# A float32 decode attention block on one core: from a tile framework with five 4 MB buffers to hand-written engine programs with two 8 MB buffers and a TensorE loop

## The chip, the core and the metric

One NeuronCore of a Trainium2 chip runs the kernel: TensorE (PE, with its weight loads listed as PEld), VectorE (DVE), ScalarE (ACT), GpSimd (POOL), SyncE (SP, which here only issues DMAs) and 16 DMA engines. The metric is the device time in microseconds of one execution. Before the change it is 381.81 us (median of 3 runs, 381.46 to 384.05).

## The reference

One token per batch row (B = 2) is normalised, goes through grouped-query attention over a cache of 4096 keys, and its result is multiplied by a gate from a small feed-forward block:

```python
xn = _layernorm(x, axis=-1)
q = (xn @ wq).reshape(B, Sq, 16, 256).transpose(0, 2, 1, 3)
k = jnp.repeat(k_cache, 2, axis=1)      # 8 heads of K and V, 4096 x 256 each
v = jnp.repeat(v_cache, 2, axis=1)
scores = jnp.einsum("bhqd,bhkd->bhqk", q, k) * (256 ** -0.5)
o = jnp.einsum("bhqk,bhkd->bhqd", softmax(scores), v)
s = o.transpose(0, 2, 1, 3).reshape(B, Sq, 16 * 256) @ wo
g = silu(((xn @ w_gate) * (xn @ w_up)) @ w_down)
return x + s * g
```

Everything is float32. K and V are 16 pieces of 4 MB each (2 batch rows times 8 heads), 134 MB together; the weights are another 24 MB. Each byte is read once.

## The kernel before

The work is 16 steps, one for each head g and batch row b (`Step`, L156). A step has one K piece and one V piece, each a tile of 128 partitions by 8192 floats (32 KB rows), which `stream` (L38) loads into a ring of five such buffers through SP's queue. The weights `wq` (two halves), `wg`, `wu` and `wd` go through the same ring; `wo` has two small buffers of its own.

The stages of a step, with the names that the profile shows:

- `scores(h)` (L179 to L191): 8 matmuls of 512 columns for each half h of the keys into `s` (L187), in four groups of 32 output partitions; DVE takes the row maximum of each half (L190).
- `softmax` (L193): the maximum over partitions by a transpose (L197), a DVE reduce `mx` (L199) and a small matmul (L202); then ACT's two exponentials `p` (L207), and `sr`, the sums (L210).
- `turn` (L213): 8 transposes of `p` into `pt` (L218), copied to `pT` by DVE and ACT (L219), and the sums' matmul (L220).
- `values(h)` (L224): 16 matmuls of 256 columns for each half into `o` (L230), then ACT's copy `ob` (L234).
- `combine` (L236): two small matmuls (L239) and DVE's scaling into `oT` (L242).

A float32 matmul with 512 or 256 columns is two MATMUL and two LDWEIGHTS rows in the profile (1024 rows of L230 for 512 calls); a transpose is one of each.

The order of instructions on each engine is that of the code, since the pools run under a manual schedule. The main loop (L273 to L304) keeps two steps in flight: it issues the loads of V for step i and of K for step i + 2, then multiplies the first half of V of step i, puts the softmax of step i + 1 between the two halves, turns step i + 1's weights, and computes the scores of step i + 2 around `combine`. The gate's matmuls (`ffn_in`, `ffn_out`) lie in steps 1 and 2, the second half of q in step 4, and the projection `project` (L255) follows each finished head. The last V piece is loaded in smaller parts with the last parts of `wo` between and behind them (`load_v_last`, L166). A load waits on SP until its ring buffer has been read by TensorE.

## Time and profile before

| what | value |
|---|---|
| median of 3 runs | 381.81 us |
| the profiled execution: span from first to last instruction | 379.9 us |
| HBM bytes read | 158.54 MB, 417 GB/s over the span |
| TensorE busy, mean granted clock | 247.3 us (65%), 0.80 |
| DVE, ACT, POOL busy | 65.4, 44.2, 1.2 us |

The page gives no separate total for the profiled execution; its span is its own time, 1.9 us under the median of the runs, and that difference is taken as the part of a run that lies outside the first and last instruction. In rows of the profile, `x16` is a count of instructions, the first number of a timeline row is its start in us from the span's start and the second its length; what stands in square brackets is the idle time ahead of it and what ended that. "DMA share" is the mean busy share of the 16 DMA engines.

### The profile page before, as it was taken

What the parts mean: (1) busy time and instruction counts of PE and PEld (TensorE: products, weight loads), DVE (VectorE), ACT (ScalarE), POOL (GpSimd) and SP (SyncE); (2) the same over time, 40 slices, a digit from 0 to 9 for tenths busy, and PEclk for the clock granted to TensorE, in tenths of its full rate; (3) what the DMA queues carried; (4) which work ended last, traced back from release to release, by engine and by line L of the source; (5) the groups of instructions that cost most, each with busy time, mean ns of one, the idle gap of its engine ahead of it and who ended that gap; (6) DMA issues with size and microseconds to landing.
All of it is one profiled execution on the core that took longest, in us unless ns stands there. A gap on an engine that the chain in (4) does not pass through costs nothing.

```text
span 379.9 us, 5146 instructions
## 1 busy us (share of the span) xinstructions
PE 247.3 (65%) x2320; PEld 111.0 (29%) x2320; DVE 65.4 (17%) x173; ACT 44.2 (12%) x103; POOL 1.2 (0%) x7
## 2 busy tenths in 40 slices
PE   0648494939656684957676577767749474947585
PEld 0112241403341331423232233414314132413153
DVE  3032120101121020102101111111202111111120
ACT  1001020300130210201102020201002020202020
POOL 1000000000000000000000000000000000000000
PEclk9996686795898886758668886888867888698889
DMA  8999999999999999999999999999999999999992
GB/s 336 438 438 433 424 419 433 440 402 449 423 436 438 404 446 420 437 428 440 425 435 423 428 427 438 426 431 412 449 426 428 433 428 426 435 432 430 416 397 100
DMA packets 7690, 158.87 MB, mean 418 GB/s; under 512 B 882, under 2 KB 1396, under 8 KB 2932
## 3 DMA queue, kind: packets, MB, share of 16 engines
q1 hardware_dynamic: 7648, 158.54, 97.7%
q8 instruction: 18, 0.29, 0.3%
q14 instruction: 4, 0.03, 0.0%
q10 hardware_dynamic: 20, 0.01, 0.0%
HBM read 158.54 MB, written 0.00 MB: 417 GB/s over the span
## 4 chain that ended last, share of the span: by engine, by line
DMA 84%; PE 14%; DVE 1%; issue 0%; SPq 0%
DMA ring<-v 45%; DMA ring<-kt 34%; PE o L230 5%; PE s L187 5%; DMA ring<-wq 3%; PE s L90 2%; DMA wo<-wo 2%; PE o L239 1%; DVE mx L199 1%; PE s L93 1%; PE sm L202 0%; PE pt L218 0%; PE pt L108 0%; PE sm L197 0%; PE acc L259 0%
## 5 line engine op out<-in xcount | busy, mean ns | idle before, releaser
L230 PE MATMUL o<-ring,pT 128*32 128x256 f32 x1024 | 91.7, 519 | 62.4 <-DMA ring<-v 62.0
L187 PE MATMUL s<-ring,qT 128*32 128x512 f32 x512 | 86.6, 813 | 36.6 <-DMA ring<-kt 36.6
L230 PEld LDWEIGHTS o<-ring,pT 128*32 128x32 f32 x1024 | 42.1, 142 | 100.8 <-issue 90.3
L207 ACT ACTIVATE p<-s,m 128x512 f32<-128x512 f32 x32 | 21.7, 682 | 257.4 <-DVE m L203 257.4
L190 DVE TENSOR_REDUCE m<-s 128x1 f32<-128x512 f32 x32 | 22.1, 691 | 115.4 <-PE s L187 115.4
L187 PEld LDWEIGHTS s<-ring,qT 128*32 128x32 f32 x512 | 16.7, 132 | 71.4 <-issue 41.6
L199 DVE TENSOR_REDUCE mx<-sm 1x128 f32<-1x512 f32 x16 | 10.9, 679 | 108.6 <-PE sm L197 108.6
L218 PE MATMUL pt<-ident,p 128*128 128x128 f32 x128 | 18.3, 284 | 1.6 <-ACT p L207 1.6
L90 PE MATMUL s<-ring,xnT 128*32 128x512 f32 (+1 forms) x96 | 12.6, 664 | 7.5 <-DMA ring<-wq 6.2
L218 PEld LDWEIGHTS pt<-ident,p 128*128 128x128 f32 x128 | 14.0, 143 | 10.2 <-ACT p L207 6.4
L239 PEld LDWEIGHTS o<-sel,ob 128*128 128x128 f32 x64 | 10.7, 238 | 21.3 <-issue 20.3
L202 PE MATMUL sm<-one,mx 1*128 1x1 f32 x32 | 7.1, 287 | 12.3 <-DVE mx L199 12.3
L219 DVE COPY pT<-pt 128x512 f32<-128x512 f32 x16 | 11.0, 691 | 14.6 <-PE pt L218 14.6
L239 PE MATMUL o<-sel,ob 128*128 128x2 f32 x64 | 12.0, 292 | 0.5 <-ACT ob L234 0.5
L219 ACT COPY pT<-pt 128x512 f32<-128x512 f32 x16 | 9.4, 585 | 10.1 <-PE pt L218 10.1
L202 PEld LDWEIGHTS sm<-one,mx 1*128 1x128 f32 x32 | 5.7, 221 | 16.3 <-DVE mx L199 16.3
L259 PEld LDWEIGHTS acc<-wo,oT 128*32 128x32 f32 x256 | 7.8, 126 | 6.7 <-issue 5.8
L259 PE MATMUL acc<-wo,oT 128*32 128x112 f32 x256 | 9.3, 286 | 0.2 <-DMA wo<-wo 0.2
L210 DVE TENSOR_TENSOR sr<-su 128x128 f32<-128x128 f32 x16 | 4.7, 292 | 26.3 <-ACT p L207 26.3
L234 ACT COPY ob<-o 128x256 f32<-128x256 f32 x16 | 6.0, 372 | 16.8 <-PE o L230 16.8
L90 PEld LDWEIGHTS s<-ring,xnT 128*32 128x32 f32 x96 | 3.2, 123 | 14.1 <-issue 11.9
L207 ACT ACTIVATION_READ_ACCUMULATOR p<-s,m 128x1 f32 x32 | 6.3, 196 | 0.0
(52 smaller groups left out, 57.9 us busy)
## 6 DMA issues: line engine op xcount, KB each, us to landing
ring<-kt SPq DMA_DIRECT2D x16, 4096.0 KB, 44.5
ring<-v SPq DMA_DIRECT2D x15, 4096.0 KB, 44.7
ring<-wq SPq DMA_DIRECT2D x2, 3584.0 KB, 28.1
wo<-wo SPq DMA_DIRECT2D x6, 896.0 KB, 46.2
ring<-wg SPq DMA_DIRECT2D x1, 3136.0 KB
ring<-wu SPq DMA_DIRECT2D x1, 3136.0 KB, 38.7
ring<-wd SPq DMA_DIRECT2D x1, 3136.0 KB, 35.5
ring<-v SPq DMA_DIRECT2D x1, 2048.0 KB, 35.9
```

The source lines that it names most:

```text
L90: nc.tensor.matmul(ps[W * c:W * (c + 1), :n], xnT[:, k, :], block(NT * k + c), start=k == 0, stop=False)
L187: nc.tensor.matmul(s[W * c:W * (c + 1), :], qT[:, self.g, self.b, d].rearrange("p r j -> p (r j)"), k[:, d, c, :], start=d == 0, stop=d == 1)
L190: nc.vector.tensor_reduce(self.m[:, h:h + 1], s, axis=AX.X, op=OP.max)
L199: nc.vector.tensor_reduce(mx, sm[:1, None, :128].rearrange("p o (c j) -> p o j c", c=NT).to_broadcast([1, NT, W, NT]), axis=AX.X, op=OP.max)
L202: nc.tensor.matmul(sm[:, 128:129], mx.rearrange("p c j -> p (c j)"), one, start=True, stop=True)
L207: nc.scalar.activation(self.p[:, h], self.s[h], AF.Exp, bias=m[:, 3:4], scale=1.0 / 16, accum_out=su[:, h:h + 1])
L218: nc.tensor.transpose(pt[:, i, :], self.p[:, h, i * 128:(i + 1) * 128], ident)
L219: (nc.vector.tensor_copy, nc.scalar.copy)[h](self.pT[:, h], pt)
L230: nc.tensor.matmul(self.o[W * c:W * (c + 1), :DH], self.pT[:, h, i, W * c:W * (c + 1)], vt[:, i, c, :], start=h == 0 and i == 0, stop=h == ...
L234: nc.scalar.copy(self.ob, self.o[:, :DH])
L239: nc.tensor.matmul(oc[:, 2 * d:2 * d + 2], self.ob[:, d * 128:(d + 1) * 128], sel, start=True, stop=True)
L259: nc.tensor.matmul(acc[W * n:W * (n + 1), :], l, wo_t[g][:, i, n * SL:(n + 1) * SL], start=g == 0 and i == 0, stop=g == HKV - 1 and i == 3)
```

## The change

The kernel is written anew for each engine, with semaphores set by hand in place of the framework. What changes in the work:

- **Loads.** Two buffers `buf` of 128 x 16384 floats (64 KB rows) take the place of the ring of five. One load brings V of step i and K of step i + 2 as one 8 MB tile (`kv`); the first brings K of steps 0 and 1; V of steps 14 and 15 come as 4 MB tiles (`vv`). The load i into a buffer is issued when TensorE has done the scores of step i, the last work on that buffer.
- **Weights.** All of the feed-forward and q weights are loaded and used ahead of the first K, as three loads (50, 25 and 56 KB rows). All of `wo` is loaded at the end in six parts, behind the last V, and all of the projection follows the last step.
- **V's product.** Each matmul takes two neighbouring key blocks, 512 columns wide: 16 matmuls for a step in place of 32. Half of each product is not wanted; `join` picks the wanted half with four small matmuls in place of `combine`'s two.
- **Order.** TensorE's step is values, turn, join, scores, then the maximum's transpose and matmul, without the softmax in the middle of values. The maximum is one DVE reduce over 1024 columns. The query operand is spread out for each step by a POOL copy into `qs`.
- **Loop.** 14 of TensorE's 16 steps are a hardware loop of 7 turns with two steps in its body; the other engines' programs are written out.
- `take` is a wait followed by a decrement of the semaphore, an instruction of its own.

TensorE before, one step in the middle of the program (`o` is V's product, `sm` the small results, `s` the scores):

```order
L230 MATMUL o<-ring,pT 32x256 x16
L197 MATMUL sm<-ident,m 1x128
L202 MATMUL sm<-one,mx 128x1
L230 MATMUL o<-ring,pT 32x256 x16
L218 MATMUL pt<-ident,p 128x128 x8
L220 MATMUL sm<-sel,sr 128x2
L187 MATMUL s<-ring,qT 32x512 x8
L239 MATMUL o<-sel,ob 128x2 x2
L187 MATMUL s<-ring,qT 32x512 x8
```

TensorE after, one step of the loop's body:

```order
L366 MATMUL o<-buf,pT 32x512 x16
L300 MATMUL pt<-ident,p 128x128 x8
L356 MATMUL sm<-sel,sr 128x2
L374 MATMUL oc<-sel,ob 128x2 x4
L344 MATMUL s<-buf,qs 32x512 x16
L348 MATMUL sm<-ident,m 1x128
L350 MATMUL sm<-one,mx 128x1
```

V's product is one block, and the maximum's transpose and matmul have moved from its middle to the end of the step.

SP's queue before, the last part of the program (each K, V or `wo` load with what it waits for; the names are semaphores of the DMA queue and of TensorE):

```order
L40 DMA ring<-kt 128x8192 [waits DMAHW4_49,PE_49]
L40 DMA ring<-v 128x8192 [waits DMAHW5_49,PE_49]
L169 DMA ring<-v 128x4096 [waits DMAHW7_49,PE_49]
L174 DMA ring<-v 128x1024
L174 DMA ring<-v 128x1024 [waits DMAHW6_49]
L174 DMA ring<-v 128x1024
L253 DMA wo<-wo 128x896 [waits DMAHW0_49]
```

SP's queue after, from the first K to the last part of `wo`:

```order
L124 DMA buf<-kv 128x16384 [waits pe]
L127 DMA buf<-kv 128x16384 [waits pe] x14
L130 DMA buf<-vv 128x8192 [waits pe] x2
L133 DMA low<-wo 128x6272
L133 DMA low<-wo 128x4032
L133 DMA low<-wo 128x1792
```

Each load of the stream now waits for one event of TensorE, and all of `wo` stands behind the last of them, which waits for the scores of step 15.

The core of the diff:

```diff
-    ring = ctx.enter_context(tc.tile_pool(name="ring", bufs=5))
-    def stream(src, size=ROW):
-        t = ring.tile([128, ROW], F32, name="ring")
-        nc.sync.dma_start(t[:, :size], src)
-        return t[:, :size]
...
+LOOPS = 7
+WO = 4 * HKV
+ABREAST = (14, 9, 4)
+DIRECT = (3, 1, 1)
+    def take(self, sem, n=1):
+        self.e.wait_ge(sem, n).then_inc(sem, -n)
...
+    buf = [sb(f"buf{i}", [128, 2 * ROW]) for i in range(2)]
+    low = sb("low", [128, 28 * FC])
...
+    def dma_side():
+        e = nc.sync
+        e.dma_start(low, wgu).then_inc(sems["gu"], 16)
+        e.dma_start(buf[1][:, :14 * D], wd).then_inc(sems["wd"], 16)
+        e.dma_start(buf[0][:, :28 * 512], wq).then_inc(sems["wq"], 16)
+        sp.after(pe, "y4")
+        e.dma_start(buf[1], kv[0]).then_inc(turns[1], 16)
+        for i in range(N - 2):
+            sp.after(pe, *(("q", 1) if i == 0 else ("s", i)))
+            e.dma_start(buf[i % 2], kv[1 + i]).then_inc(turns[i % 2], 16)
+        for i in range(N - 2, N):
+            sp.after(pe, "s", i)
+            e.dma_start(buf[i % 2][:, :ROW], vv[i % 2]).then_inc(turns[i % 2], 16)
+        for n, lo, hi in zip(won, bounds, bounds[1:]):
+            t = low[:, lo * D:hi * D] if hi <= early else late[:, (lo - early) * D:(hi - early) * D]
+            e.dma_start(t, wo[:, lo * D:hi * D]).then_inc(n, 16)
+        sp.after(dv, "res")
+        e.dma_start(out, r1).then_inc(sems["res"], 16)
...
+        po.after(dv, "qT")
+        for i in range(N):
+            g, b = where(i)
+            if i >= 2:
+                po.after(pe, "s", i - 2)
+            e.tensor_copy(qs[i % 2], qT[:, g, b, :, None, :].to_broadcast([128, 2, DUP, REP])).then_inc(sems["q"], 1)
...
+        for i in range(N):
+            ac.after(pe, "v", i)
+            e.copy(ob, o).then_inc(sems["ob"], 1)
+            if i + 1 < N:
+                half(i + 1)
+            if i + 2 < N:
+                exps(i + 2)
...
+        def maximum(i):
+            dv.after(pe, "s", i)
+            e.tensor_reduce(m[:, 0:1], s.rearrange("p h n -> p (h n)"), axis=AX.X, op=OP.max).then_inc(sems["m"], 1)
+            dv.after(pe, "m", i)
+            e.tensor_reduce(
+                mx, sm[:1, None, :128].rearrange("p o (c j) -> p o j c", c=NT).to_broadcast([1, NT, W, NT]),
+                axis=AX.X, op=OP.max).then_inc(sems["mx"], 1)
+            dv.after(pe, "x", i)
+            dv.ev(e.tensor_scalar(m[:, 1:2], sm[:, 128:129], -1.0 / 16, None, op0=OP.mult), "neg", i)
...
+        for i in range(N):
+            if i + 1 < N:
+                half(i + 1)
+            heads(i)
+            if i + 2 < N:
+                maximum(i + 2)
...
+        def scores(i, k):
+            pe.take(sems["q"])
+            k = k.rearrange("p (h d c n) -> p h d c n", h=2, d=2, c=NT)
+            for h in range(2):
+                for d in range(2):
+                    for c in range(NT):
+                        ins = e.matmul(s[W * c:W * (c + 1), h], qs[i % 2][:, d].rearrange("p j q -> p (j q)"),
+                                       k[:, h, d, c, :], start=d == 0, stop=d == 1)
+            pe.ev(ins, "s", i)
+            pe.take(sems["m"])
+            pe.ev(e.transpose(sm[:1, :128], m[:, 0:1], ident), "m", i)
+            pe.take(sems["mx"])
+            pe.ev(e.matmul(sm[:, 128:129], mx.rearrange("p c j -> p (c j)"), one, start=True, stop=True), "x", i)
+
+        def turn(i):
+            pe.take(sems["sr"])
+            for h in range(2):
+                pe.ev(turned(pt[h], p[:, h]), "t", i, h)
+            pe.ev(e.matmul(sm[:, 130:132], sr, sel[:, 0], start=True, stop=True), "u", i)
+
+        def values(i, v):
+            pe.take(turns[i % 2], 16)
+            pe.take(sems["pt"], 2)
+            v = v.rearrange("p (h i c n) -> p h i c n", h=2, i=BLK, c=2)
+            for h in range(2):
+                for j in range(BLK):
+                    for c in range(2):
+                        at = 2 * (j % 2) + c
+                        ins = e.matmul(o[W * at:W * (at + 1), :], pT[:, h, j, 64 * c + 16:64 * c + 48],
+                                       v[:, h, j, c, :], start=h == 0 and j < 2, stop=h == 1 and j >= 2)
+            pe.ev(ins, "v", i)
+
+        def join(i):
+            pe.take(sems["ob"])
             for d in range(2):
+                for h in range(2):
+                    ins = e.matmul(oc[:, 2 * d:2 * d + 2], ob[:, h * 256 + d * 128:h * 256 + (d + 1) * 128], sel[:, h],
+                                   start=h == 0, stop=h == 1)
+            pe.ev(ins, "j", i)
+
+        pe.take(turns[1], 16)
+        scores(0, buf[1][:, :ROW])
+        turn(0)
+        scores(1, buf[1][:, ROW:])
+
+        at, count = dict(pe.at), pe.n
+        with nc.Fori(0, LOOPS, 1, engines=[PE], head_slot={PE: 0}):
+            for i in range(2):
+                values(i, buf[i][:, :ROW])
+                turn(i + 1)
+                join(i)
+                scores(i + 2, buf[i][:, ROW:])
...
+        i = N - 2
+        values(i, buf[0][:, :ROW])
+        turn(i + 1)
+        join(i)
+        values(i + 1, buf[1][:, :ROW])
+        pe.after(dv, "oT", i)
+        join(i + 1)
+        pe.after(dv, "gate")
...
+        for n, lo, hi in zip(won, bounds, bounds[1:]):
+            e.wait_ge(n, 16)
             for i in range(lo, hi):
+                if i >= 4 * (HKV - 1):
+                    pe.after(dv, "oT", N - 1)
+                if i < early:
+                    ins = abreast(o, left(i), wo_step(i), i, early)
+                else:
+                    for c in range(NT):
+                        ins = e.matmul(acc[W * c:W * (c + 1), :SL], left(i), wo_step(i)[:, c * SL:(c + 1) * SL],
+                                       start=False, stop=i == WO - 1)
+            if hi == early:
+                pe.ev(ins, "w4")
+                pe.after(ac, "accs")
+                spread(False)
+        pe.ev(ins, "fin")
...
-    kt = c(k.transpose(0, 1, 7, 3, 6, 5, 4, 2)).reshape(B, HKV, 128, ROW)
-    v = c(A_v_cache).reshape(B, HKV, 128, ROW)
+    k = k.transpose(1, 0, 7, 3, 6, 5, 4, 2).reshape(N, 128, ROW)
+    v = np.asarray(A_v_cache).transpose(1, 0, 2, 3).reshape(N, 128, ROW)
+    kv = np.concatenate([np.concatenate([k[:1], v[:N - 2]]), k[1:]], 2)
+    vv = c(v[N - 2:])
...
+    wq = np.concatenate([folded(wq[:, h * 2048:(h + 1) * 2048], 512) for h in range(2)], 1)
+    wo = c(np.asarray(A_wo).reshape(WO, 128, D).transpose(1, 0, 2)).reshape(128, WO * D)
+    wgu = np.concatenate([folded(np.asarray(w), FC) for w in (B_w_gate, B_w_up)], 1)
```

## The prediction

> **What bounds the kernel now.** I read the page first (span, DMA queues, chain of waits, DMA issues), then the busy time by stretches, then SP's waits.

> ```profile
> span 379.9 us, 5146 instructions
> ...
> PE 247.3 (65%) x2320; PEld 111.0 (29%) x2320; DVE 65.4 (17%) x173; ACT 44.2 (12%) x103; POOL 1.2 (0%) x7
> ...
> q1 hardware_dynamic: 7648, 158.54, 97.7%
> q8 instruction: 18, 0.29, 0.3%
> ...
> DMA 84%; PE 14%; DVE 1%; issue 0%; SPq 0%
> ...
> ring<-kt SPq DMA_DIRECT2D x16, 4096.0 KB, 44.5
> ```

> ```profile
> 100.00:300.00 200.00, 133.64 (x1285) 61.15 (x1277) 34.61 (x89) 24.93 (x58) 0.00 (x0) 0.79 1.00 430
> 360.00:370.00 10.00, 8.27 (x101) 5.11 (x105) 2.12 (x6) 2.40 (x6) 0.00 (x0) 0.83 0.99 400
> 370.00:376.00 6.00, 5.24 (x113) 3.06 (x105) 0.23 (x1) 0.37 (x1) 0.00 (x0) 1.00 0.48 183
> ```

> In the stretches the last two numbers are the DMA share and GB/s. The kernel is bound by its stream: from 100 to 300 us the 16 DMA engines are busy all the time (1.00) at 430 GB/s, and 158.54 MB at 430 GB/s are 368.7 of the 379.9 us. At that rate one 4096 KB piece (4.19 MB) takes 9.75 us, an 8 MB tile 19.5 us. From issue to landing 44.5 us go by, so about 35 us of loads always wait ahead of a new one. That depth is the cover of everything else: SP does wait for TensorE, 88.8 us in 12 waits on V's product alone, and the stream still has no hole.

> ```profile
> SPq L40 <- PE o L230: 88.8, 12, 9.0
> ```

> So little can be gained: 379.9 less 368.7 is 11 us, and part of that is the start and the output. The question is where a queue that is only one load deep leaves holes.

> **The change, part by part.** First TensorE's step, since it now gives the signal for each load. One step of before, and at two other places the two halves of V's product:

> ```profile
> 321.67 3.64 PE L230 MATMUL o<-ring,pT 128*32 128x256 f32 x32 [5.23 <-DMA ring<-v]
> ...
> 326.90 3.64 PE L230 MATMUL o<-ring,pT 128*32 128x256 f32 x32
> ...
> 341.11 3.36 PE L230 MATMUL o<-ring,pT 128*32 128x256 f32 x32 [5.19 <-DMA ring<-v]
> 344.41 0.27 PE L197 MATMUL sm<-ident,m 128*1 128x128 f32 x1
> 345.45 0.38 PE L202 MATMUL sm<-one,mx 1*128 1x1 f32 x2 [0.77 <-DVE mx L199]
> 345.76 1.93 PE L230 MATMUL o<-ring,pT 128*32 128x256 f32 x32
> 347.62 1.09 PE L218 MATMUL pt<-ident,p 128*128 128x128 f32 x8
> 348.55 0.28 PE L220 MATMUL sm<-sel,sr 128*128 128x2 f32 x2
> 350.74 3.55 PE L187 MATMUL s<-ring,qT 128*32 128x512 f32 x16 [1.91 <-DMA ring<-kt]
> 354.22 0.63 PE L239 MATMUL o<-sel,ob 128*128 128x2 f32 x4
> 354.78 1.92 PE L187 MATMUL s<-ring,qT 128*32 128x512 f32 x16
> ```

> The same half costs 1.93 us or 3.36 to 3.64: after a wait TensorE runs at half speed at first. Scores show the same (3.55, then 1.92), so 512 columns in 16 rows cost what 256 in 32 rows cost; V's wider product therefore changes nothing but the number of weight loads, and those hide beside the matmuls. I cost it at nothing.

> A step of the change, from the landing of its load to the end of its scores: values start cold, 3.6 + 1.9 = 5.5; turn 1.1; the sums 0.3; join is four of L239's matmuls where 0.63 was two, 1.2; scores warm, 2 x 1.92 = 3.8; five waits between them, an estimate of 0.3 from the 0.02 to 0.04 us gaps in such chains and a decrement at each. Sum 12.2 us. If the whole step ran warm it would be 2 x 1.93 + 1.1 + 0.3 + 1.2 + 3.8 + 0.3 = 10.6; with all of values and half the scores cold (the 326.90 row is still slow 5 us after the start) 7.3 + 1.1 + 0.3 + 1.2 + 5.5 + 0.3 = 15.7.

> The copy of `ob` ahead of join is 512 wide on ACT, 585 ns by the row for `pT` below, beside the 1.4 us of turn and sums: nothing while these are there. The POOL copies into `qs` have a whole step of time (POOL is busy for 1.2 us in all): nothing. DVE's maximum over 1024 columns, behind the scores, is twice 691 ns at most.

> ```profile
> L190 DVE TENSOR_REDUCE m<-s 128x1 f32<-128x512 f32 x32 | 22.1, 691 | 115.4 <-PE s L187 115.4
> ...
> L219 ACT COPY pT<-pt 128x512 f32<-128x512 f32 x16 | 9.4, 585 | 10.1 <-PE pt L218 10.1
> ```

> **Steady state: nothing.** After its scores TensorE waits 1.4 us for the maximum, 0.3 for the transpose, 0.8 for `mx` (0.77 above), 0.4 for the matmul and some 0.3 for waits: 3.2. A step is 15.4 us of TensorE against 19.5 us of load, and the signal for the next load comes 12.2 us after a landing. What lies between a landing and the first byte of a load issued on its signal I take from the smallest load of the trace, on an empty queue, issued at 0.74 and used at 2.14: 1.4 us for issue, first byte and landing.

> ```profile
> 0.74 0.56 ACTq L45 DMA_DIRECT2D x<-x  x1
> ```

> ```profile
> 2.14 0.61 DVE L64 TENSOR_REDUCE st<-x 2x1 f32<-2x448 f32 x1 [0.63 <-DMA x<-x]
> ```

> So a load is queued 19.5 - 12.2 - 1.4 = 5.9 us before the one ahead of it ends. The removed depth costs nothing here, as long as TensorE's step stays under that.

> **The last V: +3.8 us (2.0 to 7.4).** Here the cover fails. V of step 14 is only 4 MB, 9.75 us, and behind it on SP stands the load of V 15, which waits for the scores of step 15; all of `wo` stands behind that wait. The scores need the tile before V 14. The stream is empty for 12.2 + 1.4 - 9.75 = 3.85 us; a warm step of 10.6 gives 2.3 (2.0 if the waits are free), and 15.7 gives 7.4. It is taken cold, since even a wait of 1.91 us (350.74) is followed by 3.55.

> [...]

> **The first pair: +1.0 us (0 to 2.5).** K of steps 0 and 1 land together, and the third tile waits for the scores of step 1 while the second (19.5 us) streams. The chain between is in the trace:

> ```profile
> 26.48 0.27 PE L197 MATMUL sm<-ident,m 128*1 128x128 f32 x1 [1.00 <-DVE m L195]
> 27.52 0.38 PE L202 MATMUL sm<-one,mx 1*128 1x1 f32 x2 [0.77 <-DVE mx L199]
> 28.95 1.43 PE L218 MATMUL pt<-ident,p 128*128 128x128 f32 x8 [1.06 <-ACT p L207]
> 30.18 0.43 PE L220 MATMUL sm<-sel,sr 128*128 128x2 f32 x2
> ```

> Scores of step 0 cold and then warm 5.5, maximum 1.4, then 26.48 to 30.61 is 4.1, 1.0 more because turn now waits for both exponentials and `sr`, scores of step 1 cold 7.1 (2 x 3.55), 1.4: 20.5 against 19.5. Warm scores make it nothing, a late start of the exponentials 2.5.

> **The start: nothing.** The stream begins with 17 MB of weights, 39 us. The gate needs the first 6.4 MB (15 us) and a few microseconds of matmuls, then K is issued while `wq` streams; q is done while K streams.

> **Fewer packets: -1.7 us (-2.2 to 0).** In the last stretch before, with small rows:

> ```profile
> q1 hardware_dynamic: 875, 1.88, 61.1%
> ```

> That is 61.1% of 16 engines in 8 us (368 to 376), 78.2 us; 1.88 MB at 430/16 GB/s are 69.9, so a packet costs 9.5 ns beside its bytes. There are 7648; in the change 27 loads of 128 rows with 16 completions each are 3900. 3750 x 9.5 ns / 16 = 2.2 us. No row here is longer than 32 KB; if 64 KB go as two packets, 1.1 are left; I take the middle.

> **Less code to fetch: -0.4 (-0.8 to 0).** 18 instruction packets hold 0.3% of the engines, 1.0 us each on one engine; spread over 16 all of them are 1.1 us. The unrolled TensorE code falls to a third.

> **Even engines: -1.5 (-3.1 to 0).** At the end of before the engines run dry one by one: a share of 0.48 over 6 us is 3.1 us lost. In the change the empty stretch at the last V lets all start anew, so the end is even, but that stretch itself begins with the slowest engine. Half.

> **The end: +0.2 (0 to 0.6).** 128 output rows in place of 8; the last `wo` part is 4 matmuls as before:

> ```profile
> 376.00 0.40 PE L259 MATMUL acc<-wo,oT 128*32 128x112 f32 x8 [0.17 <-DMA wo<-wo]
> ```

> **Sum:** 3.8 + 1.0 - 1.7 - 0.4 - 1.5 + 0.2 = +1.4 us on the profiled execution, 381.3 in place of 379.9; the median before lies 1.9 above the span, so the forecast is 381.8 + 1.4 = 383.2. The ends of all terms give -4.1 (377.7) and +10.5 (392.3).

> **Rivals.**
> *The last hole is small and the engines even out (faster).* TensorE warm at step 15 and all of the unevenness gone: +2.0 + 0 - 2.2 - 0.8 - 3.1 + 0 = -4.1, 377.7. For it: 4640 of the 5146 instructions are TensorE's, and the loop holds most of them once; against it: the steps of before start cold.
> *The holes are larger (slower).* Both halves of values and half the scores cold at step 15, the first pair late: +7.4 + 2.5 - 1.7 - 0.4 + 0 + 0.4 = +8.2, 390. The 326.90 row speaks for it.
> *The loop starves TensorE (slower).* 18 packets for TensorE's 2320 matmuls and 2320 weight loads are 258 instructions each; the body (94 calls, some 340 instructions) does not fit one, so each return to its head may fetch code again, behind 64 KB rows. Two steps leave 2 x (19.5 - 15.4) = 8.2 us; a stall beyond that is added to the time six times: 10 us give 1.8 x 6 = 11 us, 394. Against it: a fetch holds its engine for only 1.0 us.
> [...]

> **How the numbers follow.** This kernel's measurement can tell about 1% (3.8 us) from no change: 378.0 and 385.6. The forecast (380 to 387 with its own bounds) has 0.60, of which 0.08 lies over 385.6; the fast rival 0.17, of which 0.11 lies under 378.0, since a term could also be better than its bound; the larger holes 0.13; the loop 0.10. Faster 0.11, slower 0.08 + 0.13 + 0.10 = 0.31, the same 0.58. The range 377.5 to 390 leaves about 0.08 below and 0.12 above.

> **What would show it.** DMA share near 1.00 from 85 us to the end of the last 8 MB tile; an empty stretch of 3 to 6 us behind V 14, at some 345 us, ended by the scores of step 15; values of 5 to 6 us behind a wait; SP waiting for scores, not scores for SP, in the steady state; about 3900 packets; a share near 1 in the `wo` part. Wrong would be holes in every second step (the loop), or a rate away from 430 GB/s with 64 KB rows.

## The result and the profile after

The changed kernel takes 384.81 us (median of 8 runs, 382.90 to 386.71); before takes 382.00 in the runs beside it. The ratio is 1.0059 (95% interval 1.0032 to 1.0085): 0.6% slower, within the 1% that was called no change, inside the range, and on the upper side of the forecast of 383.2. The profiled execution has a span of 383.7 us against 379.9.

The page of the changed kernel, the lines that answer to those of before:

```profile
span 383.7 us, 3749 instructions
...
PE 224.3 (58%) x1642; PEld 88.4 (23%) x1642; DVE 60.3 (16%) x142; ACT 48.8 (13%) x105; POOL 5.0 (1%) x23
...
q1 hardware_dynamic: 3888, 158.59, 96.4%
q8 instruction: 5, 0.08, 0.1%
```

The share of queue 1 tells what happened. 96.4% of 383.7 us are 369.9 us of work for the mean DMA engine, 13.8 us are empty; before it was 97.7% of 379.9, 371.2 us of work and 8.7 us empty. The work became 1.3 us less, the empty time 5.1 us more, 3.8 us together.

Where the holes are, by stretches (the last two numbers are the DMA share and GB/s), first of the changed kernel, then of before at the same times:

```profile
75.00:90.00 15.00, 12.18 (x81) 4.95 (x80) 3.22 (x6) 2.55 (x6) 0.24 (x1) 0.80 0.88 347
100.00:300.00 200.00, 118.95 (x858) 48.37 (x862) 33.48 (x70) 26.18 (x60) 2.36 (x10) 0.76 1.00 432
342.00:352.00 10.00, 7.70 (x65) 3.77 (x61) 3.06 (x6) 1.42 (x3) 0.00 (x0) 0.94 0.48 177
```

```profile
75.00:90.00 15.00, 7.20 (x53) 1.58 (x49) 0.75 (x2) 0.53 (x1) 0.00 (x0) 0.82 0.99 420
...
342.00:352.00 10.00, 7.32 (x81) 3.87 (x77) 1.90 (x5) 2.40 (x6) 0.00 (x0) 0.84 0.99 424
```

A hole of 0.12 x 15 = 1.8 us at the first pair and one of 0.52 x 10 = 5.2 us at the last V, both where the prediction put them; between 100 and 300 us there is none. These shares are rough, because a stretch counts a packet whole if it begins in it, and a 64 KB row of this kernel lasts 2.42 us. Added up from the start and length of each packet of queue 1 in the trace, the mean engine is idle for 4.9 us at the last V and for 1.5 us at the first pair; before, for under 0.1 us at either. The chain of waits begins at the second hole and names its cause:

```profile
337.83 4.96 PE o L366 x32
342.79 1.02 PE pt L300 x8
343.81 0.12 PE sm L356 x2
343.93 0.89 PE oc L374 x8
344.82 3.62 PE s L344 x32
348.44 0.02 issue
348.45 0.33 SPq L130
...
349.30 25.10 DMA low<-wo
374.40 0.04 issue
374.44 4.90 PE o L305 x26
379.35 0.02 issue
379.37 0.54 ACT ys L191
```

TensorE's whole step 13 (values, turn, sums, join, scores of step 15) stands ahead of SP's issue of V 15 at 348.45. A second thing to see is at the end: the chain leaves the DMA at 374.40, and 26 rows of the projection then take 4.90 us.

In the steady state a step of the loop looks like this, after 5.6 us of waiting for its tile:

```profile
124.97 5.57 PE L366 MATMUL o<-buf,pT 128*32 128x512 f32 x32 [5.60 <-PEq L50]
130.47 1.09 PE L300 MATMUL pt<-ident,p 128*128 128x128 f32 x8
131.41 0.28 PE L356 MATMUL sm<-sel,sr 128*128 128x2 f32 x2
131.55 1.03 PE L374 MATMUL oc<-sel,ob 128*128 128x2 f32 x8
132.51 3.64 PE L344 MATMUL s<-buf,qs 128*32 128x512 f32 x32
137.59 0.27 PE L348 MATMUL sm<-ident,m 128*1 128x128 f32 x1 [1.44 <-PEq L50]
138.72 0.35 PE L350 MATMUL sm<-one,mx 1*128 1x1 f32 x2 [0.86 <-PEq L50]
```

It was forecast at 5.5, 1.1, 0.3, 1.2 and 3.8 us, and TensorE is done 14.1 us after the landing, well inside the 19.5 us of a load. The line L50 in the brackets is `take`: its wait is an instruction of TensorE's queue, so the profile names the queue and not the DMA behind it.

### The profile page after: what moved, and what is told of

It reads as the page before. It is cut to its first block, busy times and chain, and to the rows that moved or that the text cites. A ratio compares the mean times of both kernels' runs of the same rounds, so it can differ in the third digit from the quotient of the medians.

```text
span 383.7 us, 3749 instructions
## 1 busy us (share of the span) xinstructions
PE 224.3 (58%) x1642; PEld 88.4 (23%) x1642; DVE 60.3 (16%) x142; ACT 48.8 (13%) x105; POOL 5.0 (1%) x23
## 3 DMA queue, kind: packets, MB, share of 16 engines
q1 hardware_dynamic: 3888, 158.59, 96.4%
HBM read 158.54 MB, written 0.06 MB: 413 GB/s over the span
## 5 line engine op out<-in xcount | busy, mean ns | idle before, releaser
L366 PE MATMUL o<-buf,pT 128*32 128x512 f32 x512 | 87.0, 841 | 73.5 <-PEq L50 73.5
L344 PE MATMUL s<-buf,qs 128*32 128x512 f32 x512 | 60.7, 616 | 9.4 <-PEq L50 9.4
L366 PEld LDWEIGHTS o<-buf,pT 128*32 128x32 f32 x512 | 22.4, 149 | 125.0 <-issue 124.9
L242 DVE TENSOR_REDUCE m<-s 128x1 f32<-128x1024 f32 x16 | 19.6, 1225 | 65.8 <-PE s L344 65.8
L185 ACT COPY ob<-o 128x512 f32<-128x512 f32 x16 | 9.4, 586 | 136.8 <-PE o L366 136.8
L344 PEld LDWEIGHTS s<-buf,qs 128*32 128x32 f32 x512 | 15.5, 113 | 40.5 <-issue 40.3
L374 PE MATMUL oc<-sel,ob 128*128 128x2 f32 x128 | 16.5, 251 | 0.8 <-PEq L50 0.8
L374 PEld LDWEIGHTS oc<-sel,ob 128*128 128x128 f32 x128 | 15.6, 192 | 1.7 <-issue 1.7
L350 PE MATMUL sm<-one,mx 1*128 1x1 f32 x32 | 6.6, 273 | 13.8 <-PEq L50 13.8
L291 PE MATMUL s<-low,xnT 128*32 128x448 f32 x48 | 7.0, 730 | 12.5 <-DMA low<-wgu 12.5
L305 PE MATMUL o<-low,oT 128*32 128x448 f32 x54 | 8.1, 684 | 2.9 <-DMA low<-wo 2.9
## 6 DMA issues: line engine op xcount, KB each, us to landing
buf<-vv SPq DMA_DIRECT2D x2, 4096.0 KB, 14.8
```

Source lines behind the costliest of these rows:

```text
L242: e.tensor_reduce(m[:, 0:1], s.rearrange("p h n -> p (h n)"), axis=AX.X, op=OP.max).then_inc(sems["m"], 1)
L291: e.matmul(t[W * c:W * (c + 1), :n], xnT[:, k, :], block(NT * k + c), start=k == 0, stop=False)
L305: return e.matmul(t[W * c:W * (c + 1), :D], lhs, rhs, start=i < NT, stop=i >= total - NT)
L344: ins = e.matmul(s[W * c:W * (c + 1), h], qs[i % 2][:, d].rearrange("p j q -> p (j q)"), k[:, h, d, c, :], start=d == 0, stop=d == 1)
L350: pe.ev(e.matmul(sm[:, 128:129], mx.rearrange("p c j -> p (c j)"), one, start=True, stop=True), "x", i)
L366: ins = e.matmul(o[W * at:W * (at + 1), :], pT[:, h, j, 64 * c + 16:64 * c + 48], v[:, h, j, c, :], start=h == 0 and j < 2, stop=h == 1 an ...
```

## Experiments

The two holes left several readings open. At the hole behind V 14 the DMA engines don't stop together: by the packets of the trace the first runs dry at 343.9 us, half of them by 344.25 and the last at 346.8. If an edit closes a hole, does the time fall by what the mean engine lost, or only by what the slowest lost? And are the saved work and the loop worth what the sum gave them?

### V 15 issued earlier

V of step 15 overwrites V of step 13, so its load may go as soon as V's product of step 13 is done:

```diff
         for i in range(N - 2, N):
-            sp.after(pe, "s", i)
+            sp.after(pe, *(("v", i - 2) if i == N - 1 else ("s", i)))
```

> The load of V 15 waits for V's product of step 13 instead of the scores of step 15, so it is issued some 5.6 us earlier (at about 342.9 in place of 348.4). Theory A, that what counts is the mean share of the 16 DMA engines: the stretch from 342 to 352 us had a share of 0.48, so 5.2 us come back and the time is about 379.6. Theory B, that what counts is the slowest DMA engine, which ran until about 346.8 us and stood still only until about 349.5: 2.6 us come back, about 382.2. Theory C, that TensorE's projection sets the end anyway: less than 1 us.

Measured: 378.46 us, ratio to before 0.9898 (0.9877 to 0.9920), 6.3 us less than the changed kernel. The same stretch and the same place of the chain of waits in this run:

```profile
342.00:352.00 10.00, 7.51 (x69) 3.65 (x65) 3.05 (x6) 1.42 (x3) 0.00 (x0) 0.98 0.96 390
```

```profile
343.06 0.33 SPq L130
...
343.90 25.61 DMA low<-wo
369.51 0.04 issue
369.55 3.21 PE o L305 x26
```

The issue moved from 348.45 to 343.06, the landing in front of the projection from 374.40 to 369.51, 4.9 us. That is near theory A's 5.2 (and the 4.9 us of idle time by the packets); B (2.6) and C (under 1) are out. A alone leaves over 1 us unexplained. In these two executions the 26 rows behind the landing took 4.90 and 3.21 us, so 1.7 more; whether that is in the medians is asked by the last experiment.

### The first K pair as two loads

```diff
-        e.dma_start(buf[1], kv[0]).then_inc(turns[1], 16)
+        e.dma_start(buf[1][:, :ROW], kv[0][:, :ROW]).then_inc(sems["k0"], 16)
+        e.dma_start(buf[1][:, ROW:], kv[0][:, ROW:]).then_inc(turns[1], 16)
...
-        pe.take(turns[1], 16)
+        pe.take(sems["k0"], 16)
         scores(0, buf[1][:, :ROW])
         turn(0)
+        pe.take(turns[1], 16)
         scores(1, buf[1][:, ROW:])
```

> K of steps 0 and 1 come as two loads with a semaphore each, so that the scores of step 0 start some 9.7 us earlier and the signal for the third tile (scores of step 1) comes some 8 us earlier. The hole at 80 us should be gone. Theory A (mean share, 0.88 over 15 us): 1.8 us less, about 383.0. Theory B (slowest engine, idle for some 0.3 to 0.5 us there): about 384.3, no measurable change.

Measured: 381.82 us, ratio 0.9996 (0.9977 to 1.0014), 3.0 us less than the changed kernel. The stretch of the hole is full:

```profile
75.00:90.00 15.00, 6.93 (x40) 2.43 (x41) 0.46 (x2) 0.59 (x1) 0.00 (x0) 0.56 1.01 434
```

Theory B is out here too. The gain is above A's 1.8, and the traces show where more of it lies. The 64 KB rows that begin between 80 and 90 us, at and behind the hole, take 2.81 us on average in the changed kernel and 2.42 us here; for its 46 such rows that is 1.1 us of the mean engine, which counts as work and not as idle time. With the 1.5 us of idle time it makes 2.6 of the 3.0 us, and the changed kernel's own runs spread over 3.8 us.

### Smaller parts of wo at the end

```diff
-ABREAST = (14, 9, 4)
+ABREAST = (9, 5, 5, 4, 4)
```

> The early part of wo comes in five loads of 9, 5, 5, 4 and 4 blocks instead of three of 14, 9 and 4; the bytes are the same. In the changed kernel TensorE starts 13 blocks at half speed at 374.4 and ends them at 379.3, as the last bytes land, and the rest of the chain runs to 381.4. If that chain sets the end, smaller portions bring the end to about 0.5 us behind the last landing, 1.5 us less, about 383.3. If the last landing sets the end, no change (384.8).

Measured: 384.81 us, ratio 1.0059 (1.0035 to 1.0082): no change. The span of its profiled execution was 382.2, but the medians show nothing. In its trace the time saved ahead of the last matmuls is partly lost in them: the 40 rows of L419 take 2.00 us, where the changed kernel's take 1.14.

### All three edits, and without the third

The fourth run has the three edits above, the fifth the first two (the wo parts stay 14, 9 and 4).

> All three edits: V 15 waits for V's product of step 13, the first K pair comes as two loads, wo comes in smaller parts. Theory A (mean share): 5.2 + 1.8 + 1.5 = 8.5 us less, about 376.3. Theory B (slowest engine): 2.6 + 0.4 + 1.5 = 4.5 us less, about 380.3. Before is 382.0, so both would beat it.

> The two edits that close the holes (V 15 waits for V's product of step 13; K of steps 0 and 1 as two loads) with wo in its parts of 14, 9 and 4. If their gains add (6.3 and 3.0 us), 375.5; if the small wo parts of the run with all three edits helped, this is above that run's 376.1.

Measured: 376.12 us with all three, ratio 0.9839 (0.9819 to 0.9860), and 375.82 us with the two, ratio 0.9828 (0.9802 to 0.9855); beside them before took 382.19 and 383.02. The two edits' gains add (9.0 us less than the changed kernel, 6.3 + 3.0 = 9.3 by the single runs), the third gives nothing. Both versions beat before, by 1.6% and 1.7%. The queue lines of the fifth run:

```profile
q1 hardware_dynamic: 4032, 158.59, 98.3%
q8 instruction: 5, 0.08, 0.1%
```

Its span is 374.5 us: 368.1 us of work and 6.4 us empty, the start and the end. The stretch of the last V is full:

```profile
342.00:352.00 10.00, 7.52 (x52) 2.23 (x56) 2.57 (x5) 1.45 (x4) 0.00 (x0) 0.83 0.99 424
```

In this kernel the stream has no holes, so the next three ask for the terms of the work with the fifth run as their base, on the same chip.

### The loop written out

```diff
-        with nc.Fori(0, LOOPS, 1, engines=[PE], head_slot={PE: 0}):
-            for i in range(2):
-                values(i, buf[i][:, :ROW])
-                turn(i + 1)
-                join(i)
-                scores(i + 2, buf[i][:, ROW:])
...
+        for i in range(2 * LOOPS):
+            values(i, buf[i % 2][:, :ROW])
+            turn(i + 1)
+            join(i)
+            scores(i + 2, buf[i % 2][:, ROW:])
```

> As the run before, without holes, but TensorE's 14 steps written out in place of the loop. If the code that has to be fetched takes DMA time, the instruction packets go from 5 to some 14, 1.0 us each on one engine: 0.6 us more if the mean engine counts, 1 to 2 us more if the slowest counts. If the loop's return stalls TensorE where it matters, it is faster without the loop. If neither, no change.

Measured: 377.94 us, ratio 0.9879 (0.9856 to 0.9901), against 375.82: 2.1 us slower without the loop (the runs, 377.18 to 378.21 and 374.93 to 376.70, don't overlap).

```profile
q1 hardware_dynamic: 4032, 158.59, 98.1%
q8 instruction: 13, 0.21, 0.2%
```

Eight more instruction packets. The mean engine's own work grows by 0.5 to 0.7 us (98.1% of 375.9 is 368.8); the time grows by 2.1 by the medians and by 1.4 between the two traces. That is the size of the expectation's second branch, that the engines count which are hit. It is argued and not shown: the traces fit it in part, with some 0.6 us more of idle time at V 14 and in the last loads of `wo`. The kernel with the loop takes 5 packets for the whole program, the written-out one 13.

### Tiles in rows of 32 KB

```diff
-            e.dma_start(buf[i % 2], kv[1 + i]).then_inc(turns[i % 2], 16)
+            for half in (slice(0, ROW), slice(ROW, 2 * ROW)):
+                e.dma_start(buf[i % 2][:, half], kv[1 + i][:, half]).then_inc(turns[i % 2], 16)
```

TensorE's `take` in front of these tiles waits for 32.

> As the run without holes, but each 8 MB tile (except the first, which is already in two) comes as two loads of 32 KB rows. In the traces a 64 KB row takes 13 ns less than two of 32 KB: 8 rows for each engine in 14 tiles make 1.5 us more here if the size of the row is what raised the rate from 430 to 434 GB/s; no change if it was something else (less code to fetch, fewer loads of small rows).

Measured: 377.24 us, ratio 0.9860 (0.9835 to 0.9886), 1.4 us more than the base (376.96 to 377.32 against 374.93 to 376.70).

```profile
q1 hardware_dynamic: 6048, 158.59, 98.4%
q8 instruction: 5, 0.08, 0.1%
```

2016 packets more, 126 for each engine, and 98.4% of 376.0 is 370.0 us of work, 1.9 more than the base by these rounded shares. The size of the row is worth what was expected; 1.4 us over 126 packets are 11 ns each, near the 9.5 ns that the prediction took from the end of before.

### V's product in 256 columns

```diff
-            v = v.rearrange("p (h i c n) -> p h i c n", h=2, i=BLK, c=2)
+            v = v.rearrange("p (h i c n) -> p h i c n", h=2, i=BLK, c=NT)
             for h in range(2):
                 for j in range(BLK):
-                    for c in range(2):
-                        at = 2 * (j % 2) + c
-                        ins = e.matmul(o[W * at:W * (at + 1), :], pT[:, h, j, 64 * c + 16:64 * c + 48],
-                                       v[:, h, j, c, :], start=h == 0 and j < 2, stop=h == 1 and j >= 2)
+                    for c in range(NT):
+                        ins = e.matmul(o[W * c:W * (c + 1), :DH], pT[:, h, j, W * c:W * (c + 1)],
+                                       v[:, h, j, c, :], start=h == 0 and j == 0, stop=h == 1 and j == BLK - 1)
```

`join` becomes two matmuls on 256 columns of `ob`, and ACT's copy is half as wide.

> As the run without holes, but V's product in 32 matmuls of 256 columns, and two small matmuls instead of four in join. The columns streamed are the same; the weight loads double. If they hide beside the matmuls, no change (within 0.5 us). If V's product is longer, the signal for the next load has some 6 us to spare and nothing changes either; only the end of the kernel could move, by a few tenths.

Measured: 375.64 us, ratio 0.9823 (0.9801 to 0.9846), against 375.82: no change. The 512 columns bring nothing and cost nothing.

### TensorE kept busy ahead of the last wo parts

The changed kernel with its hole, and 16 transposes ahead of the wait for the second part of `wo`:

```diff
         for n, lo, hi in zip(won, bounds, bounds[1:]):
+            if lo == ABREAST[0]:
+                for _ in range(4):
+                    turned(pt[0], p[:, 0])
             e.wait_ge(n, 16)
```

> The changed kernel as it is, with 16 more transposes of p into pt (nobody reads them) ahead of the wait for the second part of wo, so that TensorE doesn't stand still for 2.7 us there. If TensorE's half speed behind that wait is part of what the hole at the last V cost (4.90 us for 26 rows, against 3.21 in the run where V 15 came earlier), these rows take 3.2 us and the time falls by 1 to 1.7 us, to about 383.3, the hole itself unchanged. If the last landing sets the end, no change (384.8). It can't be slower unless the transposes end after the landing (0.5 us at most).

Measured: 384.25 us, ratio 1.0056 (1.0034 to 1.0078). In the trace the edit did what it should:

```profile
371.16 1.97 PE L300 MATMUL pt<-ident,p 128*128 128x128 f32 x16
374.32 3.19 PE L305 MATMUL o<-low,oT 128*32 128x448 f32 x26 [1.19 <-DMA low<-wo]
```

3.19 us in place of 4.90, and a granted clock of 1.00 over these rows in place of 0.65, yet the median fell by 0.6 us with intervals that cover each other. So the slower clock at the end is real in a trace but not shown to count in the time, and it cannot be given as the cause of the rest of the first experiment's gain.

## Why the prediction was right, and where its terms were off

**What bounds the kernel.** Right. The share stays 1.00 between the holes (100 to 300 us), closing the holes brings the time down (384.81 to 375.82 us), and halving the weight loads of V's product (the run with 256 columns doubles them again) changes nothing (375.82 against 375.64 us).

**The steady state, nothing.** Right: SP waits for scores (252.7 us in 13 waits), and no hole is seen between 100 and 300 us (share 1.00). The margin of a load's signal is 19.5 - 11.2 - 1.4 = 6.9 us (from 124.97 to the end of scores at 136.15), where 5.9 was worked out.

**The last V, +3.8.** The mechanism was right, and the first experiment shows it by taking it away; the size was low. The chain was even shorter than the 12.2 us of the forecast (337.83 to 348.44, 10.6; the same number as for a warm step, though values were slow with 4.96), which should have made the term 2.3. That is nearly what the slowest engine lost: it ends V 14 at 346.8 us, and the first row of V 15 begins at 349.4. What the term left out is that the engines don't end V 14 together. The others ended it up to 2.9 us before the slowest and stood idle for 2.0 us more on average, and the restart took 0.3, 4.9 us together. The shares around the hole:

```profile
336.00:344.00 8.00, 6.17 (x44) 2.59 (x45) 0.59 (x1) 0.74 (x2) 0.00 (x0) 0.72 0.94 406
344.00:350.00 6.00, 4.56 (x41) 1.75 (x40) 1.63 (x4) 0.43 (x1) 0.00 (x0) 1.00 0.29 93
350.00:352.00 2.00, 1.14 (x7) 0.73 (x10) 0.84 (x2) 0.25 (x1) 0.00 (x0) 0.70 0.79 295
```

The 0.94 in the first row is no part of the hole: all engines are busy until 343.9 us, and the kernel without holes shows 0.97 in the same stretch.

**Even engines, -1.5.** The size was near, the reason failed. Between 355 us and the last landing of `wo` the mean engine is idle for 2.6 us before and 1.5 after, so 1.1 us were gained at the end. But the hole did not do it by letting all engines start anew: without that hole the same idle time is 1.4 us (the first experiment) and 1.7 (the fifth). What made the end more even is not shown. And the unevenness was paid at the last V, where it is most of the difference between the chain's 2.3 us and the 4.9.

**The first pair, +1.0.** Right in place, low in size: the chain from the start of the scores of step 0 (63.78) to the end of those of step 1 (80.65) took 16.9 us, with the 1.4 us less than the 19.5 of the load that covers it, and there is still a hole, 1.5 us by the packets. In the traces of the other three runs with one load for the pair it is 2.0, 1.2 and 1.3 us. Its removal gave 3.0.

```profile
63.78 5.44 PE L344 MATMUL s<-buf,qs 128*32 128x512 f32 x32 [9.39 <-PEq L50]
...
76.37 4.28 PE L344 MATMUL s<-buf,qs 128*32 128x512 f32 x32
```

**Fewer packets, -1.7.** The direction was right: 1.4 us for the rows of the K and V tiles alone. The middle was taken in case a 64 KB row goes as two packets; it goes as one (3888 packets: 27 loads of 128 rows, and 432 packets of 4 bytes in the trace, 16 for each load). Without holes the work of queue 1 is 368.1 us against 371.2 before, 3.1 less. The changed kernel got only 1.3 of it, mostly because the rows at and behind its two holes took longer: against the kernel without holes 1.1 us of the mean engine at the first pair and 0.7 at the last V. No term had that.

**Less code to fetch, -0.4.** Too small by the experiment: written out, the loop costs 2.1 us in a stream without holes, not 0.4. The division by 16 is the doubtful step, since a fetch holds one engine, for 1.0 us, and not all; that the time follows the engines that were hit is argued, not shown.

**The loop as a rival.** It went the other way. The body's code is not fetched again at each return: 5 instruction packets in all, where one packet for each return would already make 6 more. That a body of more than one packet may be fetched again at each return was the author's guess; no trace of before has a loop. The run with 256 columns shows no such fetch either: its body has some 450 instructions, an estimate of 1.75 packets by the 258 instructions to a packet of before, and its whole program has 6.

**The sum.** +1.4 us was forecast; the spans differ by 3.8 and the medians by 2.8. Split by the packets of queue 1:

| term | forecast | by the two traces |
|---|---|---|
| last V, idle | +3.8 | +4.9 |
| first pair, idle | +1.0 | +1.5 |
| fewer packets, as work of queue 1 | -1.7 | -1.6 |
| less code, as idle time in the other stretches | -0.4 | -0.4 |
| even engines, idle ahead of the last landing | -1.5 | -1.1 |
| the end, from the last landing | +0.2 | +0.4 |
| sum | +1.4 | +3.7 |

Each term came out with its sign, but all except the code came out slower than forecast, so the errors add up to 2.3 us instead of cancelling. The fourth row is idle time between 20 and 335 us, the first pair apart; putting it down to the code is not shown, though the trace of the written-out loop has 0.5 us more there than that of its base. Two things in the agreement are luck. The -1.6 holds some 3 us of gain and about 1.5 us of slow rows that nobody had foreseen. And the forecast carried the 1.9 us between span and time over to the new kernel; where both are listed, runs of before lie 1.7 to 1.9 us above their spans and runs of the changed kernel 1.3, so half a us of the 3.8 is missing from the medians for a reason that the prediction did not have.

**Open.** Of the 6.3 us of the first experiment the hole's idle time is 4.7 and the slow rows behind it 0.7 at most; of the 3.0 us of the second they are 1.5 and 1.1. What is left is within the scatter of the changed kernel. Why the rows behind the two holes took longer, what evened out the end, and whether TensorE's slower clock behind the hole counts in the time stay open.

## What to carry to other kernels

When a deep queue of loads is made shallow, look for the places where a load is smaller than the work that gives the signal for the next one: here the first and the last tiles (1.5 and 4.9 us of idle time), not the steady state (a share of 1.00). Let each load wait for the last reader of just the bytes that it overwrites, not for the end of the step: that one line was worth 6.3 us here, and with the first pair split it turned a kernel 0.6% slower than before into one 1.7% faster. Count a hole by when the DMA engines run dry one after the other (here from 343.9 to 346.8 us), not by when the last one does. And don't take a code fetch for its share of the mean engine alone: the run with eight more of them took 2.1 us longer here, where that share is 0.5, for a reason that is not shown.
